# Batch 0 of a fused attention and feed-forward kernel: tail loads on ScalarE's queue, tail rotations on GpSimd, key and value halves shared by VectorE and ScalarE

## The chip, the core and the metric

The kernel runs on one core of a Trainium2 chip. Its time is the device time of one execution in microseconds (us). In the text PE is TensorE's matrix multiply, PEld its weight load, DVE is VectorE, ACT is ScalarE, POOL is GpSimd and SP is SyncE, which issues most of the DMAs.

## What is computed

```python
def phi(x, c, s):                       # c, s: cos and sin of pi/2 * pos/S
    r = np.maximum(x, 0.0)
    return np.concatenate([r * c, r * s], axis=-1)
q_p = phi(q, cos_w, sin_w)              # q, k, v: 8 batches, 8 heads, 576 tokens, 64 columns
k_p = phi(k, cos_w, sin_w)
kv = np.einsum('bhsf,bhsd->bhfd', k_p, v)
z = np.sum(k_p, axis=2)
num = np.einsum('bhsf,bhfd->bhsd', q_p, kv)
den = np.einsum('bhsf,bhf->bhs', q_p, z)[..., None] + 1e-06
x = num / den                           # as 4608 tokens of 512 columns
h = x @ w_in                            # 512 x 2048
out = np.maximum(0.01 * h, h) @ w_out   # 2048 x 512
```

Inputs and output are float32; on the chip the matrix multiplies work on float16.

## The kernel before

The tokens of a batch are cut into a main part of 512 tokens, four to a partition (j = 0 to 3), and a tail of 64. Main parts of the eight batches are groups 0 to 7; the eight tails of q make a ninth group, while the tails of k and v belong to their own batch, because `kv` sums over all 576 tokens. For a group the steps are: rotate q, k (`phi`, two instructions for each j, the cosine half and the sine half), transpose q on PE, multiply k with v into `kv`, multiply q with `kv`, divide, transpose the result into `xT`, and run the two feed-forward layers, `ffn1` (w_in) and `ffn2` (w_out).

Nothing is scheduled by the framework: every engine takes its instructions in the order in which the Python code emits them, and waits only on semaphores. Batch 0 is written out by hand, in two halves of four heads (`hg` = 0, 1), so that PE can begin on the first half while the second is still on its way. From group 1 on the order comes from tables of positions; the change doesn't touch them.

The names that the change and the prediction use, all for batch 0:

- `load_main` loads half of the heads of q, k or v (512 KB) on SP's queue. `load_kvtail` loads a tail of k or v in two DMAs of 64 KB on the queue that it is given.
- `q_part`, `k_main`, `k_tail` are the rotations (line 240 on DVE and POOL, line 238 on ACT); `kpm` and `kpt` hold the rotated main part and tail of k. `v_main` casts v into `vmain` (line 248 on DVE and POOL, 246 on ACT). `v_tail` makes the two masked copies of v's tail in `vtail` (line 223 on DVE, 221 on ACT).
- `q_transpose` is eight transposes of one j into PSUM (line 365), `q_copy` brings them to `qpT` in SBUF (1024 columns, line 246 or 248). j = 0, 2 and 3 are rotated by DVE, j = 1 by ACT.
- `kv_half(0, hg)` is 16 matrix multiplies of `kpm` with `vmain` and 2 of `kpt` with `vtail`, for four heads, and ACT's copy of the result into `kv` (line 322). Its last argument is a number of blank multiplies (`idle`, line 164, two for each) put ahead of it, which only keep PE at work.
- `num_half(0, jp, hg)` multiplies two j of q with that `kv` (line 416), and DVE divides: `den`, `rden`, `xp` (lines 391, 395, 396). `x_transpose_half` transposes `xp` on PE (line 433) and ACT copies it to `xT` (line 437).
- `ffn1` for m = 0 to 3 is cut into halves of the tokens and chunks of w_in (line 459). `cast_w1` turns w_in to float16.

Two tables are used by ACT: one for the sine that gives `cos_t` and `sin_t`, one with the leaky ReLU; each has to be loaded before its first use (ACT_TABLE_LOAD).

Of the kernel before, what the change touches and what calls it, by code (L numbers as in the profile page):

```python
# [9 lines left out]
dt = mybir.dt  # L10
AF = mybir.ActivationFunctionType
ALU = mybir.AluOpType

P = 128
# [4 lines left out]
def kernel(  # L19
# [14 lines left out]
    nc = tc.nc  # L34
# [18 lines left out]
    def pool(name, bufs, space=None, stack=ctx):  # L53
        kw = {"space": space} if space is not None else {}
        return stack.enter_context(
            tc.tile_pool(name=name, bufs=bufs, reuse_waits="tile", **kw)
        )

    PS = bass.MemoryType.PSUM
    const = pool("const", 1)  # L60
# [19 lines left out]
    ACT, DVE, POOL = nc.scalar, nc.vector, nc.gpsimd  # L80
# [17 lines left out]
    def load_kvtail(nm, src, b, eng=nc.sync):  # L98

        t = kvtail.tile([P, H // 2, D], dt.float32, name=f"{nm}tl", tag="kvtail")  # L100
        v4 = src[b, :, MAIN:S, :].rearrange("(c o) p d -> o p c d", o=2)
        for o in range(2):
            eng.dma_start(t[o:P:2], v4[o])
        st[nm + "t", b] = t
# [51 lines left out]

    blank = const.tile([P, N2], dt.float16, name="blank")
    nc.vector.memset(blank, 0.0)  # L160

    def idle(n, ps):
        for _ in range(2 * n):
            nc.tensor.matmul(ps[:, 0:N2], lhsT=blank[:, 0:P], rhs=blank)
# [10 lines left out]
    w_ang = math.pi / 2.0 / S  # L175
    half_pi = const.tile([P, 1], dt.float32, name="half_pi")
    nc.vector.memset(half_pi, math.pi / 2.0)
    zero = const.tile([P, 1], dt.float32, name="zero")
    nc.vector.memset(zero, 0.0)
    pos = const.tile([P, J + 2], dt.float32, name="pos")  # L180
    nc.gpsimd.iota(
        pos[:, 0:J],
# [22 lines left out]
        allow_small_or_imprecise_dtypes=True,  # L205
    )
    sub_ = pos[:, J + 1 : J + 2]
    load_kvtail("k", k, 0, nc.gpsimd)
    load_kvtail("v", v, 0, nc.gpsimd)
    nc.vector.tensor_tensor(out=sub_, in0=sub_, in1=odd[:, 1:2], op=ALU.subtract)  # L210
    nc.vector.tensor_scalar(out=sub_, in0=sub_, scalar1=0.5, scalar2=None, op0=ALU.mult)
    cos_t = const.tile([P, J + 2], dt.float32, name="cos_t")
    sin_t = const.tile([P, J + 2], dt.float32, name="sin_t")
    nc.scalar.activation(cos_t, pos, AF.Sin, bias=half_pi, scale=w_ang)
    nc.scalar.activation(sin_t, pos, AF.Sin, bias=zero, scale=w_ang)
    warm = const.tile([P, 1], dt.float16, name="warm")
    nc.scalar.activation(warm, zero, AF.Lrelu)

    def masked(eng, o, i, col):
# [40 lines left out]
    def k_main(b, j, eng_c, eng_s, lo=0, hi=H):  # L260
        k_part(b, j, 0, eng_c, lo, hi)
        k_part(b, j, 1, eng_s, lo, hi)

    def k_tail(b, eng_c, eng_s):
        k_part(b, J, 0, eng_c)
        k_part(b, J, 1, eng_s)

    def k_part(b, j, part, eng, lo=0, hi=H):
        c = j if j < J else J + 1
        col, f = (cos_t, sin_t)[part][:, c : c + 1], part * D  # L270
        if j < J:
            o, i = st["kpm", b][:, lo:hi, j, f : f + D], st["k", b][:, lo:hi, j, :]
        else:
            o, i = st["kpt", b][:, :, f : f + D], st["kt", b]
        phi_half(eng, o, i, col)

    def v_main(b, lo, hi, eng):
        copy(eng, vmain[:, lo:hi, :, 0:D], st["v", b][:, lo:hi])

    def v_tail(b, eng, both=(0, 1)):  # L280
        for o in both:
            masked(eng, vtail[:, :, o, 0:D], st["vt", b], odd[:, o : o + 1])
# [34 lines left out]
    def kv_half(b, hg, where, blanks=0):  # L317
        ps = psum(where, [P, MAIN], dt.float32, "ps_kvh")
        idle(blanks, ps)
        ps = ps[:, 0 : 4 * NE]  # L320
        kv_mm(b, hg, ps)
        nc.scalar.copy(
            kv[b][:, 4 * hg : 4 * hg + 4, 0 : NE - 1],
            ps.rearrange("p (h e) -> p h e", h=4)[:, :, 0 : NE - 1],
        )
# [35 lines left out]
    def q_transpose(g, j, eng, where="h"):  # L361
        qp = st["qp", g, j]
        ps = psum(where, [P, H, P], dt.float16, "ps_qt")
        for h in range(H):
            nc.tensor.transpose(ps[:, h, :], qp[:, h, :], ident)
        st["ps_qt", g, j] = ps
        if eng is not None:
            q_copy(g, j, eng)

    def q_copy(g, j, eng):  # L370
        qpT = qptpool.tile([P, H, P], dt.float16, name="qpT")
        copy(eng, qpT, st["ps_qt", g, j])
        st["qpT", g, j] = qpT
# [33 lines left out]
    def num_half(g, jp, hg, where, blanks=0):  # L407

        if hg == 0:
            st["xp", g, jp] = qppool.tile([P, 2, H, D], dt.float16, name="xp", tag="qp")  # L410
        ps = psum(where, [P, 2, 512], dt.float32, "ps_numh")
        idle(blanks, ps[:, 0])
        for o in range(2):
            for hh in range(4):
                h = 4 * hg + hh
                nc.tensor.matmul(
                    ps[:, o, hh * NE : (hh + 1) * NE - 1],
                    lhsT=st["qpT", g, 2 * jp + o][:, h, :],
                    rhs=kv[g][:, h, 0 : NE - 1],
                )  # L420
        divide(ps, st["xp", g, jp][:, :, 4 * hg : 4 * hg + 4, :])

    def x_transpose_half(g, jp, hg, ps=None, out=True, where="o"):

        if ("xT", g) not in st:
            st["xT", g] = xtpool.tile([P, NKC, MAIN], dt.float16, name="xT")
        xp = st["xp", g, jp]
        if ps is None:
            ps = psum(where, [P, 2, 2 * P], dt.float16, "ps_xth")
        for cc in range(2):  # L430
            for o in range(2):
                h = 4 * hg + 2 * cc
                nc.tensor.transpose(
                    ps[:, cc, o * P : (o + 1) * P], xp[:, o, h : h + 2, :], ident
                )
        if out:
            nc.scalar.copy(
                st["xT", g][:, 2 * hg : 2 * hg + 2, jp * 2 * P : (jp + 1) * 2 * P], ps
            )
# [70 lines left out]
    def cast_w1(i, cp, eng, lo=0, hi=2):  # L510
        copy(eng, w1[i][cp][:, lo:hi], st["w1", i][:, 2 * cp + lo : 2 * cp + hi])
# [44 lines left out]
                q_part(0, j, part, eng, 4 * hg, 4 * hg + 4)  # L556
    q_prep(0, 3)
    kp_tiles(0)
    for j in range(3):
        k_main(0, j, DVE, DVE, 0, 4)  # L560
    v_main(0, 0, 4, DVE)
    k_tail(0, DVE, DVE)
    v_tail(0, DVE, (1,))
    for j in range(J):
        q_transpose(0, j, None, "ts"[j > 1])
        if j < 2:
            q_copy(0, j, ACT)
            idle(2, ps_idle)
    k_main(0, 3, ACT, ACT, 0, 4)
    v_tail(0, ACT, (0,))  # L570
    q_copy(0, 2, ACT)
    kv_half(0, 0, "t", 9)
    q_copy(0, 3, DVE)
    for j in range(2):
        k_main(0, j, DVE, DVE, 4, 8)
    for j in range(2, 4):
        k_main(0, j, ACT, ACT, 4, 8)
    v_main(0, 4, 6, POOL)
    v_main(0, 6, 8, POOL)
    num_half(0, 0, 0, "s", 2)  # L580
    num_half(0, 1, 0, "s")
    for c in range(2):
        cast_w1(0, 0, POOL, c, c + 1)
    for c in range(2):
        cast_w1(0, 1, POOL, c, c + 1)
    for i in range(2, NB):
        for cp in range(2):
            cast_w1(i, cp, POOL)
    kv_half(0, 1, "t", 4)
    x_transpose_half(0, 0, 0, where="t")  # L590
    num_half(0, 0, 1, "s")
    num_half(0, 1, 1, "s")
    x_transpose_half(0, 1, 0, where="t")
    half = 2 * P
    halves = ((0, half), (half, MAIN))
    for m in (0, 2):
# [3 lines left out]
                    ffn1(0, m + n, lo, hi, (c,), "s")  # L600
        x_transpose_half(0, m // 2, 1, where="t")
    for lo, hi in halves:
        for m in range(4):
            ffn1(0, m, lo, hi, range(2, 4))
    for cp in range(2):
        cast_w1(1, cp, DVE)
    start_ps.close()
# [555 lines left out]
```

## Time and profile before

| | |
|---|---|
| time, median of 3 runs | 272.02 us (271.8 to 272.48) |
| time of the profiled execution | 272.34 us |
| its span in the profile | 270.5 us |
| PE busy | 263.2 us, 97% of the span, 2668 instructions |
| PEld busy | 226.6 us, 84% |
| DVE busy | 203.6 us, 75% |
| ACT busy | 199.0 us, 74% |
| POOL busy | 13.2 us, 5% |
| granted TensorE clock | 1.0 in all slices |
| DMA | 57.05 MB, 211 GB/s on average |

The span begins with the first instruction in the trace and ends with the last; the time is 1.84 us more than the span. A row of the timeline reads: start, duration, engine, line, operation, out<-in, partitions x elements and types, count, and in brackets how long the engine had been idle before and what released it. Where a row covers several instructions, its duration runs from the first one's start to the last one's end. Instructions of one engine overlap a little, so that the distance from start to start is less than a duration.

### The profile page before, as it was taken

To read this page: it belongs to the slowest core of one execution; us is meant where nothing else is said; L and a number is where in the kernel's file an instruction comes from. 1 tells how busy PE (TensorE), PEld (TensorE's weight loads), DVE (VectorE), ACT (ScalarE), POOL (GpSimd) and SP (SyncE) were. 2 spreads that over 40 slices of the span, in tenths; PEclk is the share of its full clock that TensorE was granted. 3 is DMA by queue.
4 is the path that set the end of the run, shared out by engine and by line. 5 is a ranking of instruction groups with operands and counts; after the bars stand their busy time and mean duration, and the time that the engine had idled before them with its cause. 6 is when DMAs were issued, how large, how long until landed. Compare 5 with 4: busy or idle time off the path is not lost.

```text
span 270.5 us, 6613 instructions
## 1 busy us (share of the span) xinstructions
PE 263.2 (97%) x2668; PEld 226.6 (84%) x2668; DVE 203.6 (75%) x451; ACT 199.0 (74%) x326; POOL 13.2 (5%) x25
## 2 busy tenths in 40 slices
PE   7899999999999999999999999999999999999994
PEld 5785455765898989889999999999999989999983
DVE  5785797797976898888779788977687757545652
ACT  6756556696878897888898789878878657766720
POOL 5057001000000000000000000000000000000000
PEclk9999999999999999999999999999999999999999
DMA  7999999969999979977999899579484612200314
GB/s 228 368 393 415 392 382 373 356 143 281 285 237 280 202 214 249 363 138 251 287 199 163 276 264 239 131 220 140 78 128 167 61 41 92 85 0 2 155 41 116
DMA packets 86190, 57.05 MB, mean 211 GB/s; under 512 B 55632, under 2 KB 81232, under 8 KB 85648
## 3 DMA queue, kind: packets, MB, share of 16 engines
q1 hardware_dynamic: 85584, 55.98, 78.7%
q8 instruction: 21, 0.34, 0.5%
q10 hardware_dynamic: 448, 0.39, 0.4%
q0 software_dynamic: 128, 0.26, 0.3%
q14 instruction: 9, 0.07, 0.1%
HBM read 36.70 MB, written 9.44 MB: 171 GB/s over the span
## 4 chain that ended last, share of the span: by engine, by line
PE 75%; DVE 2%; issue 0%
PE ps_o L886 33%; PE ps_h L785 30%; PE ps_h L495 4%; PE ps_num L380 3%; PE ps_h L886 3%; PE ps_kv L289 2%; DVE gs L254 0%; PE ps_kv L298 0%; PE ps_xt L445 0%; DVE xs L396 0%; DVE wb L254 0%; DVE w L254 0%; DVE ob L251 0%; DVE qp L240 0%; DVE kpt L240 0%
## 5 line engine op out<-in xcount | busy, mean ns | idle before, releaser
L886 PEld LDWEIGHTS <-g 128*128 128x128 f16 x648 | 62.7, 98 | 7.3 <-DVE g L251 0.2
L251 DVE TENSOR_TENSOR u<-ps_h,u 128x512 f32<-128x512 f32 x52 | 35.7, 687 | 21.1 <-PE ps_h L785 19.3
L886 PE MATMUL ps_o<-w,g 128*128 128x256 f16 x352 | 51.2, 273 | 0.0
L785 PEld LDWEIGHTS <-w 128*128 128x128 f16 x416 | 44.7, 113 | 1.2
L785 PE MATMUL ps_h<-xT,w 128*128 128x256 f16 x288 | 43.3, 273 | 0.0
L805 ACT COPY u<-ps_h 128x512 f32<-128x512 f32 x52 | 30.5, 586 | 7.1 <-PE ps_h L785 7.0
L812 ACT ACTIVATE g<-u 128x1024 f16<-128x1024 f32 x26 | 27.5, 1058 | 11.1 <-DVE u L251 10.8
L798 ACT ACTIVATE g<-ps_h 128x512 f16<-128x512 f32 x52 | 31.2, 602 | 5.6 <-PE ps_h L785 5.6
L785 PEld LDWEIGHTS <-wa 128*128 128x128 f16 x312 | 33.7, 113 | 1.2
L886 PE MATMUL ps_o<-wb,g 128*128 128x256 f16 x232 | 33.5, 273 | 0.0
L785 PE MATMUL ps_h<-xw,wa 128*128 128x256 f16 x208 | 31.3, 273 | 0.0
L886 PEld LDWEIGHTS <-gs 128*128 128x128 f16 x256 | 24.9, 98 | 2.9
L904 ACT COPY ob<-ps_o 128x512 f32<-128x512 f32 (+1 forms) x32 | 18.1, 565 | 11.9 <-PE ps_o L886 10.6
L495 PE MATMUL ps_h<-xT,w 128*128 128x512 f16 (+1 forms) x104 | 24.7, 363 | 0.0
L396 DVE TENSOR_TENSOR xs<-ps_num,rden 128x512 f16<-128x512 f32 x28 | 19.3, 691 | 1.0
L886 PE MATMUL ps_o<-w,gs 128*128 128x256 f16 x120 | 17.8, 273 | 0.0
L251 DVE TENSOR_TENSOR ob<-ps_o,ob 128x512 f32<-128x512 f32 (+1 forms) x22 | 14.8, 675 | 3.8 <-ACT ob L904 1.9
L886 PE MATMUL ps_o<-wb,gs 128*128 128x256 f16 x120 | 17.5, 272 | 0.0
L795 ACT COPY ps_h<-ps_h 128x512 f32<-128x512 f32 x26 | 14.9, 572 | 2.3 <-PE ps_h L785 1.4
L254 DVE TENSOR_TENSOR gs<-g 128x1024 f16<-128x1024 f16 x16 | 11.0, 688 | 7.0 <-ACT g L812 6.9
L785 PE MATMUL ps_h<-xw,w 128*128 128x256 f16 x104 | 15.6, 273 | 0.0
L785 PE MATMUL ps_h<-xT,wa 128*128 128x256 f16 x104 | 15.6, 273 | 0.0
(115 smaller groups left out, 409.7 us busy)
## 6 DMA issues: line engine op xcount, KB each, us to landing
qst<-in_q_dram SPq DMA_DIRECT2D x7, 1024.0 KB, 6.4
out_dram<-ob SPq DMA_DIRECT2D x14, 512.0 KB, 2.8
kst<-in_k_dram SPq DMA_DIRECT2D x6, 1024.0 KB, 7.8
vst<-in_v_dram SPq DMA_DIRECT2D x6, 1024.0 KB, 6.7
w1st<-in_moe_w_in_dram SPq DMA_DIRECT2D x8, 512.0 KB, 10.2
w2st<-in_moe_w_out_dram SPq DMA_DIRECT2D x4, 1024.0 KB, 12.9
kst<-in_k_dram SPq DMA_DIRECT2D x4, 512.0 KB, 8.1
vst<-in_v_dram SPq DMA_DIRECT2D x4, 512.0 KB, 8.6
```

Source lines behind the costliest of these rows:

```text
L251: nc.vector.tensor_tensor(out=o, in0=a, in1=b, op=ALU.add)
L254: nc.vector.tensor_tensor(out=o, in0=a, in1=b, op=ALU.subtract)
L380: nc.tensor.matmul(ps[lo:hi, h // 4, (h % 4) * NE : (h % 4 + 1) * NE - 1], lhsT=qpT[:, h, lo:hi], rhs=kv[b][:, h, 0 : NE - 1],)
L396: nc.vector.tensor_tensor(out=xs, in0=ps[:, :, 0 : 4 * NE].rearrange("p a (b e) -> p a b e", e=NE)[:, :, :, 0:D], in1=rden.rearrange("p (a ...
L495: nc.tensor.matmul(ps[:, lo:hi], lhsT=w1[m // 4][c // 2][:, c % 2, m % 4 : 512 : 4], rhs=st["xT", g][:, c, lo:hi], start=(c == 0 and lo == 0),
L785: nc.tensor.matmul(bank[:, p], lhsT=w(c), rhs=st["xb", g][n][:, c], start=(fresh and p == 0 and c == 0), stop=(c == 1), skip_group_check=True,
L795: nc.scalar.copy(bank1[bj], bank1[bi])
L798: nc.scalar.activation(st["g" + nm, g][:, 2 * t : 2 * t + 2], bank1[bi], AF.Lrelu)
L805: nc.scalar.copy(st["u", g, t][:, n], bank1[bi])
L812: nc.scalar.activation(st["gt", g][:, :, 1, 2 * t : 2 * t + 2], st["u", g, t], AF.Lrelu)
L886: nc.tensor.matmul(bank[..., lo:hi], lhsT=st[G2[n], g][:, m, pair * P : (pair + 1) * P], rhs=W2[n](m)[:, lo:hi], start=(fresh and m == 0), ...
L904: nc.scalar.copy(o_at(g, half_, col, pair), bank_of(bi, pair, pair is None))
```

## The change

All of it is in batch 0, before the first feed-forward layer is under way.

1. `load_kvtail` for k and v goes from POOL's queue, where it came behind the position tables, to ACT's queue, at ACT's beginning. Ahead of the four DMAs ACT gets a dummy sine (`warm`), so that its table is loaded without waiting for the positions; `zero` is set earlier for that.
2. `k_tail` (two instructions) goes from DVE to POOL, and both instructions of `v_tail`, one of DVE and one of ACT, go to POOL too.
3. The copies of transposed q: j = 0 and 1 stay on ACT; j = 2 goes from ACT to DVE, and j = 2 and 3 now come ahead of DVE's work on k.
4. First half of heads: k's j = 2 is shared, cosine on DVE, sine on ACT; `v_main` is cut in two, heads 0 and 1 on DVE, 2 and 3 on ACT. Second half: k's j = 1 is shared, cosine on DVE (behind the first division), sine on ACT (behind its four others).
5. The second half of the first w_in chunk is cast by DVE instead of POOL.
6. PE: blank multiplies ahead of `kv_half` go from 18 to 14 and from 8 to 6; `x_transpose_half(0, 0, 0)` goes ahead of `kv_half(0, 1)`, and `x_transpose_half(0, 1, 0)` ahead of the last `num_half`; the second pass of `ffn1` for m = 0 to 3 goes chunk by chunk.

```diff
+    zero = const.tile([P, 1], dt.float32, name="zero")
+    nc.vector.memset(zero, 0.0)
     blank = const.tile([P, N2], dt.float16, name="blank")
     nc.vector.memset(blank, 0.0)
+    warm = const.tile([P, 1], dt.float16, name="warm")
+    nc.scalar.activation(warm, zero, AF.Sin)
+    load_kvtail("k", k, 0, nc.scalar)
+    load_kvtail("v", v, 0, nc.scalar)
...
-    zero = const.tile([P, 1], dt.float32, name="zero")
-    nc.vector.memset(zero, 0.0)
...
-    load_kvtail("k", k, 0, nc.gpsimd)
-    load_kvtail("v", v, 0, nc.gpsimd)
...
-    warm = const.tile([P, 1], dt.float16, name="warm")
     nc.scalar.activation(warm, zero, AF.Lrelu)
...
     kp_tiles(0)
-    for j in range(3):
-        k_main(0, j, DVE, DVE, 0, 4)
-    v_main(0, 0, 4, DVE)
-    k_tail(0, DVE, DVE)
-    v_tail(0, DVE, (1,))
+    k_tail(0, POOL, POOL)
+    v_tail(0, POOL)
     for j in range(J):
         q_transpose(0, j, None, "ts"[j > 1])
+        q_copy(0, j, (ACT, ACT, DVE, DVE)[j])
         if j < 2:
-            q_copy(0, j, ACT)
             idle(2, ps_idle)
+    for j in range(2):
+        k_main(0, j, DVE, DVE, 0, 4)
     k_main(0, 3, ACT, ACT, 0, 4)
-    v_tail(0, ACT, (0,))
-    q_copy(0, 2, ACT)
-    kv_half(0, 0, "t", 9)
-    q_copy(0, 3, DVE)
-    for j in range(2):
-        k_main(0, j, DVE, DVE, 4, 8)
+    k_main(0, 2, DVE, ACT, 0, 4)
+    v_main(0, 0, 2, DVE)
+    v_main(0, 2, 4, ACT)
+    kv_half(0, 0, "t", 7)
+    k_main(0, 0, DVE, DVE, 4, 8)
     for j in range(2, 4):
         k_main(0, j, ACT, ACT, 4, 8)
     v_main(0, 4, 6, POOL)
     v_main(0, 6, 8, POOL)
     num_half(0, 0, 0, "s", 2)
+    k_main(0, 1, DVE, ACT, 4, 8)
     num_half(0, 1, 0, "s")
-    for c in range(2):
-        cast_w1(0, 0, POOL, c, c + 1)
+    cast_w1(0, 0, POOL, 0, 1)
+    cast_w1(0, 0, DVE, 1, 2)
...
-    kv_half(0, 1, "t", 4)
     x_transpose_half(0, 0, 0, where="t")
+    kv_half(0, 1, "t", 3)
     num_half(0, 0, 1, "s")
+    x_transpose_half(0, 1, 0, where="t")
     num_half(0, 1, 1, "s")
-    x_transpose_half(0, 1, 0, where="t")
...
     for lo, hi in halves:
-        for m in range(4):
-            ffn1(0, m, lo, hi, range(2, 4))
+        for c in range(2, 4):
+            for m in range(4):
+                ffn1(0, m, lo, hi, (c,))
```

Line numbers after the change are one higher from batch 0's rotations on. On DVE, between the last rotation of q and the first division, the order before is this (`qst` and `kst` are q and k as loaded, `ktl` and `vtl` the tails, `odd` the mask):

```order
L240 TENSOR_SCALAR qp<-qst,sin_t 128x8x64
L240 TENSOR_SCALAR kpm<-kst,cos_t 128x4x64
L240 TENSOR_SCALAR kpm<-kst,sin_t 128x4x64
L240 TENSOR_SCALAR kpm<-kst,cos_t 128x4x64
L240 TENSOR_SCALAR kpm<-kst,sin_t 128x4x64
L240 TENSOR_SCALAR kpm<-kst,cos_t 128x4x64
L240 TENSOR_SCALAR kpm<-kst,sin_t 128x4x64
L248 CAST vmain<-vst 128x16x64
L240 TENSOR_SCALAR kpt<-ktl,cos_t 128x4x64
L240 TENSOR_SCALAR kpt<-ktl,sin_t 128x4x64
L223 TENSOR_SCALAR vtail<-vtl,odd 128x4x64
L248 COPY qpT<-ps_qt 128x1024
```

The same place on DVE after the change, up to the first rotation of the second half of heads:

```order
L241 TENSOR_SCALAR qp<-qst,sin_t 128x8x64
L249 COPY qpT<-ps_qt 128x1024 x2
L241 TENSOR_SCALAR kpm<-kst,cos_t 128x4x64
L241 TENSOR_SCALAR kpm<-kst,sin_t 128x4x64
L241 TENSOR_SCALAR kpm<-kst,cos_t 128x4x64
L241 TENSOR_SCALAR kpm<-kst,sin_t 128x4x64
L241 TENSOR_SCALAR kpm<-kst,cos_t 128x4x64
L249 CAST vmain<-vst 128x8x64
L241 TENSOR_SCALAR kpm<-kst,cos_t 128x4x64
```

The tail's three instructions, one k rotation and half of the v cast have left; two copies of transposed q, each waiting for its transposes, now stand ahead of k.

ACT's beginning before the change, up to its first rotation of q:

```order
L214 ACT_TABLE_LOAD
L214 ACTIVATE cos_t<-pos,half_pi 128x6
L215 ACTIVATE sin_t<-pos,zero 128x6
L217 ACT_TABLE_LOAD
L217 ACTIVATE warm<-zero 128x1
L238 ACTIVATE qp<-qst,cos_t 128x4x64
```

ACT's beginning after it:

```order
L164 ACT_TABLE_LOAD
L164 ACTIVATE warm<-zero 128x1
L103 DMA ktl<-in_k_dram 64x4x64 x2
L103 DMA vtl<-in_v_dram 64x4x64 x2
L216 ACTIVATE cos_t<-pos,half_pi 128x6
L217 ACTIVATE sin_t<-pos,zero 128x6
L218 ACT_TABLE_LOAD
L218 ACTIVATE warm<-zero 128x1
L239 ACTIVATE qp<-qst,cos_t 128x4x64
```

Four DMA issues now stand between the sine's table and `cos_t`, and all of ACT's rotations of q come behind them.

SP's first loads before the change, with what each waits for (DMAHW0 to 7 are eight semaphores that the hardware-queue DMAs use in turn; a DMA that takes one again waits for the load that had it):

```order
L93 DMA qst<-in_q_dram 128x4x256 x2
L93 DMA kst<-in_k_dram 128x4x256
L93 DMA vst<-in_v_dram 128x4x256
L93 DMA kst<-in_k_dram 128x4x256
L93 DMA vst<-in_v_dram 128x4x256
L140 DMA w1st<-in_moe_w_in_dram 128x2x512 x2
L140 DMA w1st<-in_moe_w_in_dram 128x2x512 [waits DMAHW0_49]
```

After the change, with the four tail loads among their users:

```order
L93 DMA qst<-in_q_dram 128x4x256 x2
L93 DMA kst<-in_k_dram 128x4x256
L93 DMA vst<-in_v_dram 128x4x256
L93 DMA kst<-in_k_dram 128x4x256 [waits DMAHW0_49]
L93 DMA vst<-in_v_dram 128x4x256 [waits DMAHW1_49]
L140 DMA w1st<-in_moe_w_in_dram 128x2x512 [waits DMAHW2_49]
L140 DMA w1st<-in_moe_w_in_dram 128x2x512 [waits DMAHW3_49]
```

The order of SP's loads is the same, but the second halves of k and v now wait for the two halves of q to land, and the first two loads of w_in for k's tail.

## The prediction

> **What bounds the kernel now.** I read the waits of PE first, over the whole span, because PE is busy for 97% of it. Columns: who waited for whom, us in total, times, longest.
>
> ```profile
> PE ps_idle L164 <- DVE blank L160: 1.1, 1, 1.1
> PE ps_kvh L289 <- DVE vmain L248: 0.7, 1, 0.7
> PE ps_qt L365 <- DVE qp L240: 0.6, 1, 0.6
> PE ps_num L380 <- DVE xs L396: 0.5, 1, 0.5
> PE ps_h L459 <- ACT xT L437: 0.2, 1, 0.2
> ```
>
> All but the fourth lie in the first 20 us. Behind that PE runs without a wait, but for 0.5 us near 62 us, to the end. So the kernel's time moves with the moment from which PE has feed-forward work without a gap, and I take that as the second pass of ffn1, at 19.53 us in the timeline of the first 24 us. The rows below come from that timeline. First the way from q's second half to the first `kv`:
>
> ```profile
> 0.73 1.02 SPq L93 DMA_DIRECT2D qst<-in_q_dram  x2
> 2.34 1.28 ACT L214 ACT_TABLE_LOAD   x1 [2.34 <-DVE ones L226]
> 4.61 0.35 DVE L240 TENSOR_SCALAR qp<-qst,cos_t 128x256 f16<-128x256 f32 x1 [1.77 <-DMA qst<-in_q_dram]
> 5.55 0.49 ACT L238 ACTIVATE qp<-qst,cos_t 128x256 f16<-128x256 f32 x1
> 5.85 0.35 DVE L240 TENSOR_SCALAR qp<-qst,cos_t 128x256 f16<-128x256 f32 x1
> 8.08 1.06 PE L365 MATMUL ps_qt<-ident,qp 128*128 128x128 f16 x16
> 9.35 0.35 DVE L240 TENSOR_SCALAR kpm<-kst,cos_t 128x256 f16<-128x256 f32 x1 [1.56 <-DMA kst<-in_k_dram]
> 9.61 0.35 DVE L240 TENSOR_SCALAR kpm<-kst,sin_t 128x256 f16<-128x256 f32 x1
> 11.03 0.69 DVE L248 CAST vmain<-vst 128x1024 f16<-128x1024 f32 x1
> 11.78 0.67 PE L289 MATMUL ps_kvh<-vmain,kpm 128*128 128x65 f16 x16 [0.68 <-DVE vmain L248]
> 12.16 0.35 DVE L223 TENSOR_SCALAR vtail<-vtl,odd 128x256 f16<-128x256 f32 x1
> 12.43 0.68 DVE L248 COPY qpT<-ps_qt 128x1024 f16<-128x1024 f16 x1
> 12.57 0.29 PE L298 MATMUL ps_kvh<-vtail,kpt 128*128 128x130 f16 x2
> 12.90 0.38 ACT L322 CAST kv<-ps_kvh 128x260 f16<-128x260 f32 x1 [0.66 <-PE ps_kvh L298]
> ```
>
> The reader is to see that DVE has the last word: it waits 1.56 us for k, works without a pause from 9.35, casts v by 11.72, and PE starts the first `kv` at 11.78. PE's tail multiplies then wait until 12.57 for DVE's `vtail` (ready at 12.51), and ACT has `kv` at 13.28. Then the second half of heads:
>
> ```profile
> 13.17 0.51 ACT L238 ACTIVATE kpm<-kst,cos_t 128x256 f16<-128x256 f32 x1
> 13.33 0.67 PE L416 MATMUL ps_numh<-kv,qpT 128*128 128x65 f16 x16
> 13.58 0.50 ACT L238 ACTIVATE kpm<-kst,sin_t 128x256 f16<-128x256 f32 x1
> 13.71 1.27 POOL L248 CAST vmain<-vst 128x512 f16<-128x512 f32 x2 [9.28 <-DMA vst<-in_v_dram]
> 13.81 0.70 DVE L240 TENSOR_SCALAR kpm<-kst,sin_t 128x256 f16<-128x256 f32 x1
> 13.83 1.03 PE L164 MATMUL ps_kvh<-blank 128*128 128x256 f16 x8
> 14.70 0.81 PE L289 MATMUL ps_kvh<-vmain,kpm 128*128 128x65 f16 x16
> 15.67 0.38 ACT L322 CAST kv<-ps_kvh 128x260 f16<-128x260 f32 x1 [0.79 <-PE ps_kvh L298]
> 16.10 0.67 PE L416 MATMUL ps_numh<-kv,qpT 128*128 128x65 f16 x16
> 16.57 0.15 DVE L391 TENSOR_SCALAR den<-ps_numh 128x8 f32<-128x8 f32 x1
> 16.71 0.40 PE L433 MATMUL ps_xth<-ident,xp 128*128 128x128 f16 x4
> 16.94 0.60 PE L459 MATMUL ps_h<-xT,w 128*128 128x256 f16 x4
> 16.99 0.69 DVE L396 TENSOR_TENSOR xp<-ps_numh,rden 128x512 f16<-128x512 f32 x1
> 17.78 0.60 PE L459 MATMUL ps_h<-xT,w 128*128 128x256 f16 x4 [0.24 <-ACT xT L437]
> 19.53 4.71 PE L459 MATMUL ps_h<-xT,w 128*128 128x256 f16 x29
> ```
>
> From the first `kv` (13.28) to the second (15.67 + 0.38 = 16.05) it takes 2.77 us, and from there to 19.53 another 3.48.
>
> **The change part by part.** I follow the same chain through the new order.
>
> *To the first `kv`, with q landing as before.* The transposes of j = 2 and 3 end at 8.08 + 1.06 = 9.14, those of j = 2 half way, at 8.61. New on DVE are two copies ahead of k: a copy lasts 0.68, and neighbours on DVE overlap by 0.09 (9.35 + 0.35 against 9.61), so the next instruction starts some 0.60 behind it. They start at 8.65 and 9.25, and DVE is free for k at 9.85. In the old order it was free earlier, but waited for k until 9.35. So the copies, moved into that idle time, overrun it by 0.5 us. Five k rotations (one fewer) at 0.26 each (9.35 to 9.61) end the series at 11.15. Half the v cast has no row; between 0.35 for 256 columns and 0.69 for 1024 I estimate 0.46, which gives 11.61, and PE starts 0.06 later, at 11.67, instead of 11.78. ACT's share of k and v, three rotations at 0.41 from k's landing and half a cast, ends near 11.2 and is covered by DVE; v is needed no earlier than before. The tail of k and v no longer holds PE if POOL is done by 12.1, and that wait goes: 16 multiplies hold PE for 0.50 (13.33 to 13.83), and 0.33 behind the tail's start (12.57 to 12.90) ACT copies: 11.67 + 0.50 + 0.33 = 12.50, `kv` is there at 12.88. Gain: 0.40.
>
> POOL's four tail rotations have no row either. Its casts of 512 columns take 1.27 / 2 = 0.64; I take 0.45 for 256 columns, bounds 0.35 (DVE's) and 0.64. Four are 1.8, from the landing of the tails on; they end by about 9 and are hidden. If they took five times that, they would be PE's next wait.
>
> *From the first `kv` to the second.* What was late last here was ACT's fourth rotation and DVE's; ACT now has five, at 0.41 (13.17 to 13.58), the first starting 0.11 before `kv` is complete: 12.77 + 4 x 0.41 + 0.50 = 14.91. But something new is later. `x_transpose_half(0, 0, 0)` now stands ahead of `kv_half(0, 1)` on PE, so the second `kv` queues behind the first division: PE's multiply at 12.93, division 0.47 later (16.10 to 16.57), its end 1.11 after that (16.57 to 16.99 + 0.69), so 14.51; the transposes 0.06 later hold PE for 0.23 (16.71 to 16.94); six blanks, at (14.70 - 13.83) / 8 = 0.109, hold it for 0.65. The second `kv` starts at 15.45 instead of 14.70, ACT copies 0.83 later, and it is there at 16.66 instead of 16.05. Loss so far: 0.61. The blanks, which cost nothing before, are on the path here.
>
> *From there to the second pass.* Between 16.10 and 19.53 PE has two gaps: 16.60 to 16.71 (the division ends at 16.65) and 16.94 + 0.44 = 17.38 to 17.78 (ACT's copy of xT). In the new order `x_transpose_half(0, 1, 0)` comes ahead of the last multiplies, its division is long done, and ACT has its copy 0.1 after PE wants it. So of 0.51 about 0.13 stays: 16.71 + 3.05 = 19.76. Net: +0.23, say +0.25. The chunk order of the second pass and DVE's cast of half a w_in chunk cost nothing: DVE does the cast behind the second division, near 16.2, and PE wants it at about 17.5; without that cover it would be 0.4.
>
> *What the tail loads do to q.* Here is the largest term. First the loads' sizes and us from issue to landing, from the DMA view of the first 20 us. Then two rows of the windows of one us each: length, busy us of PE, PEld, DVE, ACT and POOL, clock, DMA share, GB/s. Last the timeline's row of three DMAs that ACT issues near the kernel's end.
>
> ```profile
> qst<-in_q_dram SPq DMA_DIRECT2D x2, 512.0 KB, 4.2
> ktl<-in_k_dram POOLq DMA_DIRECT2D x2, 64.0 KB, 6.3
> vtl<-in_v_dram POOLq DMA_DIRECT2D x2, 64.0 KB, 7.0
> ```
>
> ```profile
> 2.00:3.00 1.00, 1.00 (x7) 0.69 (x6) 0.76 (x6) 0.66 (x1) 1.00 (x2) 1.00 0.74 200
> 3.00:4.00 1.00, 1.00 (x6) 0.70 (x5) 0.00 (x0) 0.99 (x3) 1.00 (x3) 1.00 1.05 373
> ```
>
> ```profile
> 265.42 2.19 ACTq L920 DMA_DIRECT2D out_dram<-ob  x3
> ```
>
> POOL issues the tails behind its tables and they take over 6 us, so they land behind q. ACT can begin when SP does, at 0.73; with its table under way and the dummy sine handed over, I let the issues start at 1.0, an estimate. At 2.19 / 3 = 0.73 each they end by 3.9: they fall into the time in which q is on its way, with the DMA engines full from 3 us on. Their 4 x 64 KB = 0.26 MB at 373 GB/s are 0.70 us. Bounds: 0 if they fit into the engines' free quarter between 2 and 3 us, and 2.2 if they cost what lies between the landing of q's second half and of k's first (9.35 - 5.85 = 3.50) over what lies between q's halves (5.85 - 4.61 = 1.24). I take 0.70, from the nearest rate. DVE's whole chain above hangs on q's second half, so it is paid in full: +0.25 + 0.70 = +0.95.
>
> ACT itself: from the end of its first table to its first rotation of q it needs 5.55 - 2.34 - 1.28 = 1.93. That now follows the issues, 3.9 + 1.93 = 5.8, 0.3 later. It is hidden by q being 0.70 later; alone it would cost 0.3. SP's second halves of k and v now wait for q to land, but at that time k and v's first halves keep the engines full, and nothing in the chain wants them before 12; with k and v ahead of them free of tails they land earlier rather than later. That gives no gain, as DVE and not k's landing is last now.
>
> **Rivals.**
>
> *R1, q isn't delayed.* The tails use the free quarter, or trickle in between q's packets. Against it: 1.05 of the DMA engines' share is in use from 3 us. Then +0.25, or +0.55 with ACT ready 0.3 late: about 272.4, no change to be measured. Chance 0.15.
>
> *R2, the DMA issues wait for the table.* I let ACT issue while its table loads. No row of this trace has a DMA issue behind a running ACT instruction. If it can't, the issues begin at 0.73 + 1.28 = 2.0 and end at 4.9, and ACT is ready for q at 6.9, 1.3 later; the transposes of j = 1 wait for ACT, and the chain goes with them: 0.25 + 1.3 = +1.55, 273.6. Chance 0.14. The Trainium skill, PSUM — Partial Sum Buffer, section Engine vs sequencer instructions, says that a sequencer waits for earlier instructions only to be handed to the engine, not to finish; that speaks against R2 and for the forecast's 273.0, but no run here shows it for a table load.
>
> *R3, POOL blocks DVE.* DVE's k rotation at 13.81 took 0.70 instead of 0.35, while POOL's cast of 13.71 was at work. Four new POOL rotations fall among DVE's ten on q. Each could cost DVE 0.35, 1.4 in all, of which the wait of 0.9 before its copies takes up most: +0.4 on top, 273.4. Chance 0.11. The Trainium skill, SBUF — State Buffer, section SBUF: two separate sides, states that VectorE in a two-port mode and GpSimd lock a shared port pair for a whole instruction, and the other blocks; the row at 13.81 agrees with it. By that rule it would be 273.4, without it 273.0.
>
> *R4, faster: DVE's relief counts.* DVE runs from 9.35 past 16.99 all but without a pause, and loses two tail rotations, one masked copy, two k rotations (5 x 0.26) and half a v cast (0.3), 1.6 us; half a w_in cast (0.4) comes back. If q's copies are over before k lands, so that k and v set the pace, -0.9 on the way to 19.53 is possible: 271.1. It decides when DVE is free for k by about 8.9 instead of 9.85. For it: k should land earlier without tails in its way. Against it: the copies wait for the transposes, which end at 9.14. Chance 0.10.
>
> **How the numbers follow.** The profiled execution took 272.34; +0.95 makes 273.3 of it. Against the median of the runs, 272.02, it is 272.97, and I say 273.0. A measurement of this kernel can tell about 0.3%, 0.8 us, from no change. The forecast's own chance is 0.50, spread from 272.4 to 273.5 by the bounds on q's delay; about 0.16 of it lies under +0.8. Faster: R4, 0.10. Same: R1 and that part, 0.31. Slower: the rest of the forecast, R2 and R3, 0.59. The range leaves out R4's lower part and the costliest ends of R2 and R3: 271.9 to 274.2.
>
> **What would show it.** In the profile after: q's second half landing near 6.5 instead of 5.85 (the forecast) or not (R1); ACT's first rotation of q near 5.8 (forecast) or 6.9 (R2); DVE's rotations of q stretched beside POOL's (R3); the first multiply of `kv` near 12.4, the second `kv` near 17.4, its six blanks right ahead of it; the second pass of ffn1 at 20.5. I'd be wrong if PE's second pass starts before 19.5, or if the time moves by other than what that start moves.

## The result, and the profile after

| | before | after |
|---|---|---|
| median | 271.95 us (6 runs, 271.31 to 272.48) | 274.31 us (6 runs, 273.81 to 275.3) |
| profiled execution | 272.34 us | 274.36 us |
| its span | 270.5 us | 272.6 us |

The ratio is 1.0091, with a 95% interval of 1.007 to 1.0113: slower by 2.4 us. The forecast was 273.0, with a range up to 274.2. The direction was right, the size was not, and the time lies just above the range.

The waits of PE over the whole span of the kernel after, columns as before:

```profile
PE ps_kvh L290 <- DVE vmain L249: 1.8, 1, 1.8
PE ps_idle L170 <- DVE blank L162: 1.1, 1, 1.1
PE ps_xth L434 <- DVE xp L397: 1.0, 1, 1.0
PE ps_qt L366 <- DVE qp L241: 0.7, 1, 0.7
PE ps_num L381 <- DVE xs L397: 0.5, 1, 0.5
PE ps_numh L417 <- ACT kv L323: 0.5, 1, 0.5
```

The wait for DVE's cast of v ahead of the first `kv` has grown from 0.7 to 1.8 us, and the wait for the first division (`xp`) is new. The same chain as in the prediction, from the timeline of the kernel after, down to the first `kv`:

```profile
0.71 1.28 ACT L164 ACT_TABLE_LOAD   x1 [0.71 <-PEq L1148]
0.89 1.44 ACTq L103 DMA_DIRECT2D ktl<-in_k_dram  x2
5.69 0.49 ACT L239 ACTIVATE qp<-qst,cos_t 128x256 f16<-128x256 f32 x1
6.79 0.35 DVE L241 TENSOR_SCALAR qp<-qst,cos_t 128x256 f16<-128x256 f32 x1 [1.00 <-DMA qst<-in_q_dram]
7.88 1.77 POOL L241 TENSOR_SCALAR kpt<-ktl,cos_t 128x256 f16<-128x256 f32 x1 [6.02 <-ACT qp L239]
9.66 1.14 POOL L241 TENSOR_SCALAR kpt<-ktl,sin_t 128x256 f16<-128x256 f32 x1
9.66 1.29 DVE L249 COPY qpT<-ps_qt 128x1024 f16<-128x1024 f16 x2 [0.94 <-PE ps_qt L366]
10.79 1.86 POOL L224 TENSOR_SCALAR vtail<-vtl,odd 128x256 f16<-128x256 f32 x2
10.87 0.53 DVE L241 TENSOR_SCALAR kpm<-kst,cos_t 128x256 f16<-128x256 f32 x1
11.32 0.54 DVE L241 TENSOR_SCALAR kpm<-kst,sin_t 128x256 f16<-128x256 f32 x1
11.78 0.56 DVE L241 TENSOR_SCALAR kpm<-kst,cos_t 128x256 f16<-128x256 f32 x1
12.26 0.53 DVE L241 TENSOR_SCALAR kpm<-kst,sin_t 128x256 f16<-128x256 f32 x1
12.71 0.33 DVE L241 TENSOR_SCALAR kpm<-kst,cos_t 128x256 f16<-128x256 f32 x1
12.97 0.41 DVE L249 CAST vmain<-vst 128x512 f16<-128x512 f32 x1
13.43 0.67 PE L290 MATMUL ps_kvh<-vmain,kpm 128*128 128x65 f16 x16 [1.83 <-DVE vmain L249]
14.26 0.38 ACT L323 CAST kv<-ps_kvh 128x260 f16<-128x260 f32 x1 [2.53 <-PE ps_kvh L299]
```

The reader is to see two things. q's second half is rotated from 6.79 on, where it was 5.85. And as long as POOL works on the tails, until 10.79 + 1.86 = 12.65, DVE's rotations of k take 0.53 to 0.56 us and start 0.46 apart; the one at 12.71, behind POOL's last, takes 0.33 again, and the cast follows it 0.26 later. Then the second half:

```profile
16.33 0.40 PE L434 MATMUL ps_xth<-ident,xp 128*128 128x128 f16 x4 [0.97 <-DVE xp L397]
16.56 0.82 PE L170 MATMUL ps_kvh<-blank 128*128 128x256 f16 x6
17.22 0.67 PE L290 MATMUL ps_kvh<-vmain,kpm 128*128 128x65 f16 x16
18.04 0.38 ACT L323 CAST kv<-ps_kvh 128x260 f16<-128x260 f32 x1 [0.69 <-PE ps_kvh L299]
21.54 2.77 PE L460 MATMUL ps_h<-xT,w 128*128 128x256 f16 x20
```

From the first `kv` (14.64) to the second (18.42) it is 3.78 us, and 3.12 from there to the second pass at 21.54: 6.90 together, against 6.25 before (13.28 to 19.53). The second pass comes 2.01 later than before. Behind it PE's rows keep that distance up to about 68 us, where 0.35 is added, as the last part shows. PE's last row starts at 267.00 instead of 264.64, 2.36 later; what follows it is 0.26 shorter, so that the span grows by 2.1.

### The profile page after: what moved, and what is told of

Read it like the earlier page. It is cut to its first block, busy times and chain, and to the rows that moved or that the text cites. A ratio compares the mean times of both kernels' runs of the same rounds, so it can differ in the third digit from the quotient of the medians.

```text
span 272.6 us, 6600 instructions
## 1 busy us (share of the span) xinstructions
PE 263.2 (97%) x2662; PEld 226.3 (83%) x2662; DVE 204.4 (75%) x448; ACT 199.3 (73%) x328; POOL 14.7 (5%) x24
## 4 chain that ended last, share of the span: by engine, by line
PE 90%; DMA 4%; DVE 3%; ACT 1%; issue 0%; SPq 0%; ACTq 0%
PE ps_o L887 33%; PE ps_h L786 29%; PE ps_h L496 5%; PE ps_h L460 5%; PE ps_o L476 5%; DMA qst<-in_q_dram 4%; PE ps_h L887 3%; PE ps_num L381 2%; PE ps_kv L290 2%; PE ps_qt L366 1%; PE ps_kvh L290 1%; DVE kpm L241 1%; PE ps_numh L417 1%; PE ps_xth L434 1%; PE ps_kv L299 1%; DVE xp L397 1%
```

## The experiments

Every kernel ran 12 times (`i_old_second_pass` 11 times), in three sets of four beside the kernel before, whose medians there were 272.16 (a, b, d, e), 272.1 (c, g, i, j) and 272.03 us (k, m, n, e2). The changed kernel was not run again with them, so every distance to its 274.31 compares sets. The numbers in brackets behind a time are the ratio to the kernel before of the same set and its 95% interval; that ratio is not the quotient of the two medians, and in the set of c, g, i and j it is the lower of the two (1.0062 against 1.0082 for i). I call the kernels by their first letters. The table gives what the timelines of the profiled executions show: start of DVE's first rotation of q's second half, of its first rotation of k, end of the first `kv` copy, start of the second pass, and start of PE's last row.

| kernel | median | q | k | `kv` | second pass | `kv` to pass | last row |
|---|---|---|---|---|---|---|---|
| before | 272.1 | 5.85 | 9.35 | 13.28 | 19.53 | 6.25 | 264.64 |
| after | 274.31 | 6.79 | 10.87 | 14.64 | 21.54 | 6.90 | 267.00 |
| a_no_rotations | 273.19 | 7.71 | 11.79 | 14.77 | 21.67 | 6.90 | 267.16 |
| b_no_tails | 273.15 | 5.79 | 9.87 | 12.85 | 19.75 | 6.90 | 265.49 |
| g_rot_back | 273.75 | 6.64 | 10.72 | 14.00 | 20.90 | 6.90 | 266.04 |
| k_only_ktail_pool | 273.18 | 6.39 | 10.47 | 13.46 | 20.36 | 6.90 | 265.81 |
| i_old_second_pass | 274.32 | 7.14 | 11.22 | 14.71 | 21.61 | 6.90 | 266.90 |
| c_old_pe_order | 273.69 | 7.83 | 11.91 | 15.02 | 21.85 | 6.83 | 266.95 |
| m_old_order_old_k | 272.84 | 6.15 | 10.23 | 14.03 | 20.17 | 6.14 | 265.29 |
| j_blanks | 272.53 | 5.82 | 8.95 | 12.87 | 19.75 | 6.88 | 265.37 |
| d_parts_1_2 | 272.21 | 6.16 | 8.68 | 13.70 | 19.84 | 6.14 | 264.95 |
| e_loads_only | 271.66 | 6.18 | 8.78 | 12.69 | 18.95 | 6.26 | 264.06 |
| e2_loads_only | 271.42 | 7.03 | 8.88 | 13.32 | 19.46 | 6.14 | 264.57 |
| n_loads_ktail_pool | 271.67 | 6.43 | 8.76 | 12.73 | 18.87 | 6.14 | 263.99 |

Three columns carry the result. In the eight rows with the new order of DVE, q's copies ahead of k (after, a, b, g, k, i, c, m), k follows q at a fixed distance, 4.08 us; in the four with the old order and the loads on ACT (d, e, e2, n) it does not. `kv` to pass is 6.83 to 6.90 where k's j = 1 is late on DVE (the same rows but m), and 6.14 to 6.26 where it is not; j's 6.88 comes from its eight added blanks. And q is at 6.15 to 7.83 in all with the tail loads on ACT, at 5.79 to 5.85 in the three without (before, b, j).

A fourth reading is the distance from q to `kv`, in which POOL's price lies. It is 7.06 in a and b, which leave the rotations out, 7.07 in k, 7.36 in g and 7.85 in the changed kernel. With POOL's four rotations as in the change (m, after, i, c) it is 7.88, 7.85, 7.57 and 7.19, as q comes at 6.15, 6.79, 7.14 and 7.83: the later q is, the later DVE reaches k, and the more of POOL's work is over by then. So a late q hides part of POOL's price: between m and c q moves by 1.68 and `kv` by 0.99.

### a_no_rotations: the tails' rotations left out

```diff
-    kp_tiles(0)
-    k_tail(0, POOL, POOL)
-    v_tail(0, POOL)
```

Four lines near the kernel's start, not shown, make k's tiles earlier and set `kpt` and the data columns of `vtail` to zero on DVE.

> The changed kernel, but the tails of k and v of batch 0 are loaded and not rotated: kpt and vtail are set to zero by DVE early, so batch 0's tail is left out of kv. Theory S (the sum: 0.25 us from the new order, 0.9 from q landing late, 0.8 from POOL's rotations holding up DVE's rotations of k): DVE's k rotations start 0.26 apart again instead of 0.46, the first kv multiply comes near 12.6 instead of 13.43, the second pass of ffn1 near 20.7 instead of 21.54, time 273.5 us. Rival N (k's rotations are slow for another reason, such as k's late landing or DMA writes): distance stays 0.46, time stays 274.3.

273.19 us, ratio 1.003 (1.0008 to 1.0053): 1.1 under the changed kernel. DVE's rotations of k start at 11.79, 12.05, 12.31, 0.26 apart:

```profile
11.79 0.34 DVE L245 TENSOR_SCALAR kpm<-kst,cos_t 128x256 f16<-128x256 f32 x1
12.05 0.34 DVE L245 TENSOR_SCALAR kpm<-kst,sin_t 128x256 f16<-128x256 f32 x1
```

So POOL's rotations are what spreads them. The profiled execution had q at 7.71 and was the slowest of its twelve, so its second pass (21.67) says nothing on the median.

### b_no_tails: the tail loads left out as well

```diff
-    load_kvtail("k", k, 0, nc.scalar)
-    load_kvtail("v", v, 0, nc.scalar)
```

> As the run without rotations, but the tails of k and v of batch 0 are not loaded either (batch 0's tail is left out of kv). Theory S: q's second half lands at 5.8 again instead of 6.8, the first kv multiply comes near 11.7, the second pass near 19.8, time 272.2 us. Rival O (the new order itself, with DVE's copies of q ahead of k and the blanks behind the division, costs most): second pass stays beyond 20.5, time 273 us or more.

273.15 us, 1.0031 (1.001 to 1.0051). The second pass, 19.75, is within 0.05 of the prediction's sum for a q that isn't delayed (+0.25). But the time is 1.0 over before and not 0.2: PE's last row is 0.85 late, and 0.6 of it arises near 69 us, told below. The median is that of a, but that does not say that the loads cost nothing: behind the second pass b's profile loses 0.63 and a's 0.38, and a's is of its slowest run. What the loads cost in a typical run of the new order stays open.

### e_loads_only and e2_loads_only: the kernel before, with the loads on ACT alone

The dummy sine and the two `load_kvtail` lines of the change, nothing else; the second is the first once more.

> The kernel before, with only the tail loads moved to ACT's queue behind a dummy sine (part 1 of the change). Theory S: q's second half lands near 6.8, but in the old order DVE waits for k anyway until about 9.6, so only 0.2 to 0.3 us are paid: first kv multiply near 12.0, time 272.2 us. Rival P (q's delay is paid wherever it happens): +0.9, time 272.9 us.

> The kernel before with its tail loads issued by ScalarE at the beginning and nothing else, once more: whether its gain of 0.5 us is one. With VectorE's rotations of k first in the row they wait for k's landing and not for q's, so a later q costs nothing there: 271.7 again. Rival: 272.1, the first result was chance.

271.66 (0.9981, 0.9958 to 1.0003) and 271.42 (0.9979, 0.9954 to 1.0003): not slower, and likely 0.5 us faster, though neither interval alone excludes no change. Neither theory of the first run had it faster than before. In e2 q's second half came as late as 7.03, and DVE's rotations of k still began at 8.88: in the old order q's lateness runs into the time in which DVE waits for k. It is not free, though. A later q makes PE's transposes and the 18 blanks behind them later: in both kernels the first `kv` multiply follows the blanks without a wait, at 12.11 in e2 and at 11.27 in e, and the second pass is at 19.46 against 18.95. As to the gain, DVE starts on k at 8.78 and 8.88 against 9.35 before; but j, whose tail loads stand in POOL's queue as before, has 8.95, so how much of it comes from the loads' place is not shown.

### d_parts_1_2: the loads on ACT and the rotations on POOL, in the old order

As e, with `k_tail` and both parts of `v_tail` on POOL ahead of DVE's work on k.

> The kernel before, with the tail loads on ACT's queue and the tail rotations on POOL (parts 1 and 2 of the change), the rest in the old order. Theory S: POOL's rotations, some 1 us each from 7.9 to 12.7, hold up DVE's rotations of k (0.46 apart instead of 0.26), first kv multiply near 13.0 instead of 11.78, PE's wait for vtail is gone, kv near 14.1 instead of 13.28: time 272.8 us. Rival Q (DVE's relief of 0.8 us makes up for it): time 272.0 us.

272.21 (0.9999, 0.9977 to 1.002): no sign of the gain of the loads, though this interval overlaps those of e. In the profiles `kv` is there at 13.70, 1.01 later than in e. From the timelines of POOL and PE:

```profile
10.54 2.41 POOL L224 TENSOR_SCALAR vtail<-vtl,odd 128x256 f16<-128x256 f32 x2 [0.77 <-DMA vtl<-in_v_dram]
13.00 0.28 PE L299 MATMUL ps_kvh<-vtail,kpt 128*128 128x130 f16 x2 [0.98 <-POOL vtail L224]
```

POOL needs 1.2 us for each masked copy here, and PE waits 0.98 for them; in the changed kernel DVE is late enough to hide that. Neither theory had this wait. Theory S had the way to `kv` wrong: DVE starts on k at 8.68, its six rotations take 1.94 instead of 1.58 (before: 9.35 to 10.93 at 0.26 each), and the first `kv` multiply comes at 11.35, not near 13.0.

### g_rot_back: all of the change but the rotations on POOL

```diff
-    k_tail(0, POOL, POOL)
-    v_tail(0, POOL)
...
     v_main(0, 2, 4, ACT)
+    k_tail(0, DVE, DVE)
+    v_tail(0, DVE, (1,))
+    v_tail(0, ACT, (0,))
```

> The changed kernel with the tails' rotations back where the kernel before has them: k's tail and one half of v's on VectorE behind v's cast, the other half on ScalarE. All work is done. Theory S: GpSimd's part in the rotations costs 1.1 us (what leaving them out gave), and on VectorE the three tail rotations stand behind the half cast of v at 0.26 us each, so some 0.4 us comes back as a wait for the tails: VectorE's k rotations are 0.26 apart, second pass at 20.1 to 20.5, time 273.5. Rival H, leaving the rotations out helped because work was left out and not because GpSimd runs beside VectorE: the rotations of k stay 0.46 apart or the wait for the tails takes all of it, and the time is 274.3.

273.75 (1.0048, 1.0023 to 1.0073), 0.56 under the changed kernel, whose interval it just touches: DVE's rotations of k are 0.26 apart, and three tail rotations come behind the cast. From q to `kv` it is 7.36 instead of 7.85, so with all work done about 0.5 us is saved; that is less than a's 1.1, since DVE now does the tails.

### k_only_ktail_pool: only k's tail on POOL

As g, but `k_tail` stays on POOL at its old place.

> The changed kernel with k's tail still rotated by GpSimd and v's tail back on VectorE (one half, behind v's half cast) and ScalarE (the other). All work is done. Theory O, what costs is GpSimd running in the same stretch as VectorE's rotations of k: without v's tail GpSimd is done at about 10.8, before those begin, they are 0.26 us apart instead of 0.46, and the main part of the first kv multiply comes about 0.7 us earlier than the changed kernel's at the same landing of q; one tail rotation and ScalarE's half come behind it: time 273.4. Rival H, GpSimd costs by its length whatever it runs beside: it is slower than the kernel with all rotations back, over 273.75, since its rotations now lengthen those of q.

273.18 (1.0039, 1.0022 to 1.0057), 1.13 under the changed kernel and 0.57 under g, whose interval overlaps this one. POOL and DVE in its timeline:

```profile
8.70 1.14 POOL L241 TENSOR_SCALAR kpt<-ktl,sin_t 128x256 f16<-128x256 f32 x1
10.47 0.34 DVE L241 TENSOR_SCALAR kpm<-kst,cos_t 128x256 f16<-128x256 f32 x1
10.73 0.35 DVE L241 TENSOR_SCALAR kpm<-kst,sin_t 128x256 f16<-128x256 f32 x1
```

POOL ends at 9.84, before DVE's first rotation of k, and that one takes 0.34. POOL did lengthen one rotation of q (0.62 at 7.45 instead of 0.48), but behind it DVE waits for the transposes anyway, and from q to `kv` it is 7.07 as without any rotations. So it is not POOL's work as such that costs, but POOL's work in the stretch in which DVE sets the pace. Theory O holds; rival H falls by these rows more than by the times.

### c_old_pe_order and m_old_order_old_k: TensorE's order, and k's late share

c puts `kv_half(0, 1, "t", 4)` back ahead of the transposes. m does that and, besides:

```diff
-    k_main(0, 0, DVE, DVE, 4, 8)
+    for j in range(2):
+        k_main(0, j, DVE, DVE, 4, 8)
...
     num_half(0, 0, 0, "s", 2)
-    k_main(0, 1, DVE, ACT, 4, 8)
```

> The changed kernel with TensorE's old order around the second kv (kv_half(0, 1) with eight blanks first, then x_transpose_half(0, 0, 0), the two numerators, x_transpose_half(0, 1, 0)). Theory S, the change's cost as a sum of shares: from the first kv cast's end to the second pass the changed kernel took 6.90 us (14.64 to 21.54) and the kernel before 6.25 us (13.28 to 19.53), and the order is all of that 0.65; so with the order undone the second pass starts at about 20.9 and the time is about 0.65 us under the changed kernel's 274.3: 273.7. Rival W, the order costs nothing because the second kv multiply waits for k's second-half rotations anyway: second pass at 21.5, time 274.3.

> The changed kernel with TensorE's old order around the second kv and, besides, VectorE rotating the second half of k's j = 1 in one piece with j = 0, ahead of the division of the first numerator, as in the kernel before. Theory K: with the old order alone the second kv multiply waited for that rotation (from the end of the first kv cast to the second pass 6.82 us, of 6.90 in the changed kernel and 6.25 before); with both undone it is 6.25, and the time 0.57 under the 273.69 of the old order alone: 273.1. Rival D, the two rotations now hold up the division by as much: 273.7.

c: 273.69 (1.004, 1.0013 to 1.0067). The time is what was expected, but not for the reason: `kv` to pass is 6.83, so up to the second pass undoing the order alone is worth 0.07, and there rival W is right. Half of the 0.62 between the medians may be the wait near 69 us (0.35 in the changed kernel, told below), which c doesn't have; the rest is open, as c's profile, with q at 7.83, is of the slowest of its runs. PE's rows of c, with the DVE row that they wait for, and PE's row of m:

```profile
16.44 0.19 PE L290 MATMUL ps_kvh<-vmain,kpm 128*128 128x65 f16 x1
16.57 0.59 DVE L241 TENSOR_SCALAR kpm<-kst,cos_t 128x256 f16<-128x256 f32 x1
17.31 0.64 PE L290 MATMUL ps_kvh<-vmain,kpm 128*128 128x65 f16 x15 [0.67 <-DVE den L392]
```

```profile
15.46 0.81 PE L290 MATMUL ps_kvh<-vmain,kpm 128*128 128x65 f16 x16
```

In c PE starts the second `kv` 1.42 us after the first is there, as before the change, but after one multiply it stands until 17.31: DVE has k's j = 1 at 17.16 (the trace names the instruction behind it, `den`, as the releaser). In m, with that rotation back ahead of the division, the sixteen go through, 6.14 is reached, and the time is 272.84 (1.0029, 1.0012 to 1.0045). Theory K holds: k's late share alone holds the second pass by all but 0.07. PE's new order with k's j = 1 rotated early was not run, so what the order would cost by itself is open.

### i_old_second_pass and j_blanks: the loss near 69 us

i is the changed kernel with the second pass of `ffn1` in its old order; j is the kernel before with 16 blanks ahead of the second `kv` instead of 8.

> The changed kernel with the second pass of the first group's ffn1 in its old order (for each row block its two chunks, not the chunks outermost). Theory O, the added loss behind the second pass (+0.35 us in the changed kernel: the second transposing store 4.8 us instead of 2.6, the wait of ScalarE for q near 69 us) comes from the changed order of the second pass: it is gone, time 273.9. Theory P, it comes with the later second pass whatever the order: it stays, time 274.3, as the second pass starts at the same 21.5. If instead the second pass must now wait for the second chunk of the input weights that VectorE casts, the time is over 274.5.

> The kernel before with eight more blank matmuls ahead of the second kv multiply (16 where it had 8), nothing else: a pure delay of some 0.87 us at 0.11 us each. Both theories expect the second pass at 20.4 instead of 19.53. Theory T, a delay of the second pass is carried to the end and nothing is added: time 0.87 us over before, 273.0. Theory P, behind a second pass that comes over about 0.3 us later the second of the transposing stores of q (issued near 57 us) takes 4.7 us instead of 2.6, the next load of q lands 0.5 to 1 us later than the shift, ScalarE waits for it with a copy of xT queued behind, and TensorE's first matmul of the third matmul stage (near 68.5 us) loses a further 0.35 to 0.6 us: time 273.3 to 273.6, with a wait on xT at that matmul. Should the blanks lie in time in which TensorE waits anyway, both fall: time 272.1.

i: 274.32 (1.0062, 1.0039 to 1.0085). The order of the second pass is worth nothing up to that pass (6.90 as before), and 0.18 us of the loss behind it is still there. j: 272.53 (1.0006, 0.9983 to 1.003), with the second pass at 19.75 only, since the first `kv` came 0.41 earlier in that profile and the eight blanks added 0.63, not 0.87, behind it; it lost 0.5 us between 80 and 104 us, at no wait that the profile names, so it tells neither theory apart.

What happens near 69 us, from the kernel after: rows of SP and of ACT, then the matmul row of PE that needs the copy of `xT`.

```profile
56.87 6.48 SPq L347 DMA_TRANSPOSE qpT<-qp  x4
63.45 0.54 SPq L93 DMA_DIRECT2D qst<-in_q_dram  x1
69.64 0.72 ACT L239 ACTIVATE qp<-qst,cos_t 128x512 f16<-128x512 f32 x1 [0.43 <-DMA qst<-in_q_dram]
70.27 0.57 ACT L447 COPY xT<-ps_xt 128x512 f16<-128x512 f16 x1
70.89 1.36 PE L887 MATMUL ps_o<-w,g 128*128 128x256 f16 x11
```

The same places before:

```profile
54.85 5.70 SPq L346 DMA_TRANSPOSE qpT<-qp  x4
60.65 0.54 SPq L93 DMA_DIRECT2D qst<-in_q_dram  x1
67.16 0.72 ACT L238 ACTIVATE qp<-qst,cos_t 128x512 f16<-128x512 f32 x1
67.78 0.57 ACT L446 COPY xT<-ps_xt 128x512 f16<-128x512 f16 x1
68.56 1.47 PE L886 MATMUL ps_o<-w,g 128*128 128x256 f16 x12
```

The last row of the first block is cut off where its window ends, at 72 us, so its count of 11 is no difference. The four transposing stores take SP 0.78 longer, the next load of q is issued 2.80 later than before instead of 2.02, ACT waits for it and is 2.48 later, with a copy of `xT` queued behind, and PE's row comes 2.33 later instead of 2.01. In b the same row of PE shows it:

```profile
69.37 1.47 PE L886 MATMUL ps_o<-w,g 128*128 128x256 f16 x12 [0.42 <-ACT xT L449]
```

It costs some 0.35 in the changed kernel, as much in a, 0.6 in b, 0.2 in i and k (which loses 0.16 more near 98 us), and nothing in c, g, m, d, e, e2 and n. A later second pass does not bring it about (c is later than all), and with the order of that pass undone (i) the stores are as slow. But the fourteen profiles fall into two sets by another part of the change, PE's order around the second `kv`: the four stores take SP 6.48 to 6.84 us in the six kernels with the new one (after, a, b, g, k, i) and 5.41 to 6.09 in the eight with the old one (before, c, m, d, e, e2, n, j). How an order near 17 us reaches stores near 56 us is not shown. Slow stores alone are not the loss either: g has 6.50 and loses nothing, its load of q having landed 5.8 us after its issue, against 6.1 in the changed kernel.

### n_loads_ktail_pool: what could beat both

e with `k_tail` on POOL.

> The kernel before with the tail loads issued by ScalarE at the beginning, and k's tail alone rotated by GpSimd ahead of everything of k; v's tail and all the rest as before. It takes 0.52 us of tail rotations from VectorE's row between v's cast and the first kv multiply's tail. Theory O: GpSimd runs beside VectorE's rotations of q and the first of k (k lands at 8.7 to 9.4), stretches those by 0.2 each, and is done by 10: first kv multiply 0 to 0.3 later, its tails up to 0.3 earlier, time 271.4 to 271.9, at or a little under the loads alone. Rival H, its 0.2 us per rotation eats all of it: 272.1.

271.67 (0.9983, 0.9967 to 0.9999): as fast as e, and at this size of difference no better than it. DVE's relief of two tail rotations (0.52) does not show in `kv`, 12.73 against 12.69 in e: with POOL beside them DVE's six rotations of k take 1.94 here too. So of the whole change the loads on ACT are the part to keep, if any: likely 0.2% under before, and 2.6 to 2.9 us under the changed kernel.

## Why the prediction was wrong, step by step

*To the first `kv`, with q as before: right.* b has it without tails: 12.85, where the prediction had 12.88.

*POOL's four rotations, 0.45 each and hidden by about 9: this step failed.* They took 1.77, 1.14 and twice 0.93, began at 7.88 and ended at 12.65. The bounds, 0.35 to 0.64, came from POOL's casts and DVE's rotations; none was a row of POOL doing this operation, and none was taken beside a busy DVE. The prediction asked only when POOL would be done, with PE's tail multiply behind it as the next wait. What it cost was DVE: from 10.87 to 12.71 four rotations take 1.84 instead of 1.04, +0.80. a, g and k show that it goes when POOL's work leaves that stretch. Rival R3 had the mechanism, but set it among DVE's rotations of q and at +0.4, with a chance of 0.11; as POOL started at 7.88 and was slow, it met those of k. Of q's, the two last ran beside POOL's first rotation, at 7.85 and 8.24, and took 0.48 each, as before the change. The Trainium skill, SBUF — State Buffer, section SBUF: two separate sides, has a lock between GpSimd and a VectorE operation in a two-port mode, which blocks the loser for the whole instruction. The trace agrees that the two engines hold each other up, but a rotation of DVE lost 0.2 us here beside POOL instructions of 0.93, less than a full block; in which mode the rotations run no run shows.

*q delayed by 0.70, paid in full: nearly right.* It was 0.94 in the profiled execution, and the fixed 4.08 us from q to k in the new order show that it is paid in full up to k. Behind that a late q takes from POOL's price, as the distances from q to `kv` show, so that the two terms do not simply add from run to run. That 0.70 came so near is partly luck: the size varies from 0.3 to 2.0 over the eleven profiles with these loads on ACT, and a against b shows 0.04 between medians.

*First to second `kv` 2.77 to 3.78, then 3.48 to 3.10: right, 3.78 and 3.12.* The reason was half of it. The prediction laid the loss to the place of `kv_half(0, 1)` behind the first division. c shows that k's late share on DVE holds the second pass nearly as long without that (6.83 of 6.90), and only with both undone, in m, is it 6.14; what the order costs by itself is open.

*Chunk order of the second pass at nothing: right* (i).

*Behind the second pass nothing changes: wrong by 0.35*, the wait near 69 us. The prediction's own sign of being wrong, a time that moves by other than the second pass, came up here: that pass moved by 2.01 and PE's last row by 2.36. All profiles that lose time there are of kernels with PE's new order and its slower stores; the way from one to the other stays open.

The sum, for this one profiled execution: 0.95 forecast, + 0.80 for POOL, + 0.24 for q, + 0.35 behind, is 2.34; PE's last row came 2.36 later.

*The other rivals.* R2 fell: ACT issues its DMAs from 0.89, while its table loads from 0.71 to 1.99, and ACT's first rotation of q was at 5.69 (forecast 5.8). That row agrees with what the Trainium skill says in PSUM — Partial Sum Buffer, section Engine vs sequencer instructions. R1 fell for the profiled execution, R4 altogether: DVE was free for k at 10.87, not at 8.9.

## What to carry to other kernels

Before work goes from a busy engine to an idle one, ask what the idle one does to the busy one while both run, and not only whether it is done in time: here POOL was off the path and still cost 0.8 us, because it ran in the stretch in which DVE set the pace, while half of that work, over before that stretch began (k), cost nothing from q to `kv`. An operation without a row on the engine that is to get it has no upper bound from another engine's row. And where an engine waits for one input, putting work on a second input ahead of it turns every delay of that second input into time, as q's did here.

## What the runs showed of the hardware

- A POOL rotation or masked copy of 128x256 took 0.93 to 1.81 us beside DVE (the longest in m). In the changed kernel four of DVE's rotations of k took 0.53 to 0.56 beside POOL instead of 0.35; not every one is slowed (in n every second one of the first four: 0.35, 0.57, 0.34, 0.48). DVE's copies out of PSUM were not slowed: two took 1.29 at 9.66 with POOL at work, and 1.29 in a without it.
- With four loads of 64 KB issued by ACT among SP's, DVE's first rotation of q's second half spread from 6.15 to 7.83 us over eleven profiles; in the three without such loads on ACT it was at 5.79 to 5.85.
- ACT issued DMAs while it loaded a table: issues from 0.89, the load from 0.71 to 1.99.
- Four transposing stores of the same size took SP 5.41 to 6.09 us in eight kernels and 6.48 to 6.84 in six others, which differ from them only in batch 0, the first 25 us.
